# Sink values of two head pairs as two row tiles, and q and k loaded in rows of four tokens, in a fused attention and channel-mix kernel

## The chip, the cores and the metric

The kernel runs on one core of a Trainium2 chip. The metric is device time in microseconds for one execution, as the median of several runs; less is better. The engines are named as in the profile: PE is TensorE, DVE is VectorE, ACT is ScalarE, POOL is GpSimd, SP is SyncE (which issues nearly all DMAs). PEld is the weight load of TensorE, which overlaps its products.

## What is computed

Four batches of eight heads, 768 tokens, head size 64. Each token attends to the last 128 tokens up to itself and to four "sink" tokens at the start. The heads' outputs, side by side, are the 512 features of a channel mix with a shift by one token.

```python
def attention(q, k, v, n_sink=4, window=128):          # q, k, v: (4, 8, 768, 64)
    scores = q @ k.transpose(0, 1, 3, 2) / sqrt(64)
    rel = pos[:, None] - pos[None, :]
    keep = (pos[None, :] < n_sink) | ((rel >= 0) & (rel < window))
    a = softmax(where(keep, scores, -1e9))
    return a @ v

def channel_mix(x, mu_k, mu_r, w_k, w_v, w_r):          # x: (4, 768, 512)
    xk = mu_k * x + (1 - mu_k) * x_prev                 # x_prev: x one token earlier
    xr = mu_r * x + (1 - mu_r) * x_prev
    k = maximum(xk @ w_k, 0)                            # (512, 1024)
    return sigmoid(xr @ w_r) * (k * k @ w_v)            # (512, 512), (1024, 512)
```

All inputs and the output are float32; inside, the products are in bfloat16.

## The kernel before

**Units.** The work is cut into 12 units: a batch `b` and a block `T` of 256 tokens, `u = 3 b + T`. A unit is prepared (`prepare`), attended (`attend`), turned and mixed (`mix`), and sent through the two weight matrices and the gate (`ffn`). Stages of neighbouring units overlap.

**Preparation.** SP loads q, k and v in float32 (`load`). A cast makes them bfloat16 (`kb`, `qb` at L587 and L590, `vb` at L638). Then q and k are turned, so that head size lies on partitions and tokens along the row. For the units in `KD` (k of units 4 to 11) and `QD` (q of units 8 to 11) SP issues DMA transposes (L603). For the others TensorE transposes into a PSUM bank (L616) and ACT or DVE copies to `kt` or `qt` (L624). These last units load two tokens of a head as one row of 512 bytes (L403): partition `p` holds tokens `2p` and `2p + 1`, and the copy at L624 puts them in order by writing with a step of two. The others and v load rows of 256 bytes (L386, L396).

**Attention.** Heads are taken two at a time, as four "chunks" `c`. The scores (L701) use TensorE as two row tiles of 64 rows, one for each head of the chunk, and two chunks follow each other (`TOGETHER`). ACT takes the exponent (L737) and DVE multiplies with the window mask (L751). For blocks `T > 0` the sinks are computed apart: `sink_scores` (L678) gives the scores of all eight heads with their four sinks in one bank, on column tiles of 32; ACT makes `es` of it (L685), whose rows `32 c` to `32 c + 31` belong to chunk `c`. `vsink` holds the sinks' values, with zeros wherever row and head don't belong together, so that a product over all 128 rows of `es` gives the right sum for a chunk. `values` issues for each chunk and each half `g` of the tokens this sink product (L763) and then the products with the window's values (L775), all into one PSUM bank. DVE divides by the sum (L788, L791).

**Mix and weights.** `mix` transposes x on TensorE (L814), copies it out (L823), subtracts the shifted x (L841) and forms xk and xr (L852, all DVE). `ffn` issues the product with w_k (L902), the relu (L912 on ACT, L916 on DVE), the square (L924), the gate (L933), its tanh on ACT (L939), the product with w_v (L951) and the last multiplication on DVE (L960); L967 stores. The last half block has its own form (L872, L882). The weights are loaded at the start and cast (L552 to L558).

**What sets the order.** All operations are recorded in a `Plan`, each with a number. `ORDER` lists for every engine by hand which number follows which. `CHOICE` says for the operations that may run on several engines (casts, copies out of PSUM, relu) which engine takes them. `schedule` walks along these lists with costs written into the kernel, gives out the buffers and puts "fill" products (L971, `warm`) into gaps of TensorE in the first 22 us, which only keep it busy. On the chip every engine works its own list strictly in order, so an instruction that waits holds up everything behind it. PSUM has eight banks: four for the two score tiles and a pool of four, `bank`, for everything else.

Of the kernel before, what the change touches and what calls it, by code (L numbers as in the profile page):

```python
# [9 lines left out]
BF16 = mybir.dt.bfloat16  # L10
AX = mybir.AxisListType
AF = mybir.ActivationFunctionType
ALU = mybir.AluOpType
# [5 lines left out]
    79: "ACT", 82: "ACT", 83: "ACT", 85: "ACT", 87: "ACT", 89: "DVE", 94: "DVE", 95:  # L19
    "DVE", 97: "DVE", 101: "DVE", 102: "DVE", 128: "DVE", 134: "DVE", 136: "DVE", 137:  # L20
    "DVE", 140: "ACT", 141: "DVE", 150: "DVE", 191: "DVE", 192: "ACT", 193: "ACT", 218:
    "DVE", 265: "DVE", 273: "DVE", 278: "DVE", 305: "DVE", 343: "DVE", 346: "DVE", 348:
    "DVE", 352: "ACT", 354: "DVE", 361: "DVE", 423: "DVE", 429: "ACT", 430: "ACT", 499:
    "DVE", 501: "DVE", 504: "DVE", 507: "DVE", 508: "ACT", 520: "DVE", 586: "ACT", 587:
    "ACT", 654: "DVE", 658: "DVE", 660: "DVE", 663: "DVE", 672: "DVE", 736: "DVE", 738:
    "ACT", 739: "DVE", 744: "DVE", 751: "DVE", 815: "DVE", 816: "ACT", 825: "DVE", 885:
    "DVE", 887: "DVE", 891: "ACT", 892: "ACT", 1003: "DVE",
# [13 lines left out]
TOGETHER = 2  # L41

SWITCH = 100.0
# [8 lines left out]
        90, 93, 106, 96, 99, 104, 117, 77, 109, 114, 132, 138, 142, 129, 125, 120, 156,  # L52
        135, 158, 149, 184, 190, 169, 236, 208, 209, 212, 213, 220, 221, 161, 166, 172,
        177, 216, 194, 181, 201, 217, 187, 238, 291, 299, 292, 295, 300, 303, 249, 304,
        226, 296, 241, 246, 307, 224, 228, 277, 232, 229, 252, 261, 233, 267, 257, 311,
        264, 284, 270, 312, 319, 344, 309, 315, 330, 316, 349, 367, 375, 368, 376, 322,
        371, 395, 327, 372, 333, 338, 397, 275, 353, 379, 360, 380, 383, 408, 385, 387,
        422, 388, 445, 453, 446, 454, 400, 427, 405, 475, 411, 416, 391, 431, 392, 457,
        438, 458, 449, 473, 486, 450, 463, 526, 530, 527, 531, 500, 538, 461, 505, 539,
        469, 510, 470, 554, 478, 483, 534, 494, 489, 535, 512, 565, 557, 465, 579, 466,  # L60
        542, 519, 544, 562, 550, 584, 573, 551, 588, 546, 568, 632, 602, 547, 603, 606,
        614, 607, 595, 630, 643, 615, 620, 610, 618, 611, 640, 635, 678, 682, 679, 683,
        664, 646, 690, 706, 708, 686, 651, 687, 691, 626, 671, 719, 711, 622, 627, 694,
        623, 761, 757, 765, 758, 762, 766, 722, 696, 741, 727, 716, 775, 785, 702, 750,
        769, 743, 770, 796, 703, 788, 793, 698, 773, 699, 817, 777, 781, 778, 782, 835,
        831, 839, 832, 836, 799, 840, 859, 861, 843, 804, 847, 844, 824, 855, 849, 869,
        864, 872, 856, 907, 915, 908, 851, 916, 852, 880, 875, 911, 893, 912, 919, 900,
        920, 935, 937, 923, 925, 931, 948, 932, 973, 940, 974, 981, 945, 982, 951, 977,
        959, 978, 956, 985, 927, 966, 986, 928, 991, 989, 1001, 1009, 1005, 1002, 1013,
        1006, 1014, 1010, 993, 1021, 997, 994, 998, 1017, 1019, 1022, 1029, 1025, 1030,  # L70
        1026,
    ),
    "DVE": (
        69, 70, 89, 94, 95, 101, 97, 108, 102, 113, 110, 115, 111, 78, 137, 105, 116, 119,
        128, 124, 144, 126, 121, 134, 122, 127, 136, 150, 145, 151, 152, 146, 153, 191,
        147, 160, 148, 165, 80, 81, 154, 171, 141, 176, 162, 163, 167, 173, 168, 178, 174,
        179, 155, 196, 197, 203, 198, 205, 204, 211, 218, 199, 223, 206, 207, 84, 240,
        245, 305, 200, 86, 242, 306, 243, 247, 215, 248, 256, 219, 88, 278, 251, 294, 298,
        279, 230, 253, 302, 254, 234, 258, 259, 280, 265, 343, 286, 348, 281, 282, 287,
        289, 346, 321, 288, 313, 326, 317, 273, 337, 290, 323, 332, 324, 328, 283, 329,  # L80
        334, 339, 335, 340, 370, 354, 276, 374, 355, 361, 358, 362, 382, 356, 378, 364,
        357, 363, 423, 389, 399, 404, 410, 401, 415, 406, 402, 366, 412, 417, 407, 418,
        413, 359, 365, 448, 433, 393, 434, 440, 435, 442, 441, 456, 460, 499, 482, 477,
        504, 452, 529, 501, 488, 507, 436, 493, 511, 437, 471, 479, 480, 484, 444, 485,
        495, 556, 496, 490, 541, 491, 443, 537, 558, 572, 514, 559, 561, 533, 467, 515,
        520, 563, 521, 564, 517, 567, 574, 522, 575, 516, 523, 590, 552, 569, 591, 570,
        518, 525, 548, 524, 654, 634, 593, 639, 597, 660, 599, 658, 592, 598, 605, 645,
        636, 641, 637, 642, 650, 600, 617, 601, 613, 666, 647, 594, 609, 648, 652, 710,
        653, 669, 663, 667, 693, 668, 712, 672, 673, 675, 674, 676, 713, 628, 681, 624,
        670, 736, 721, 715, 726, 723, 724, 677, 685, 728, 729, 689, 760, 717, 742, 718,  # L90
        764, 792, 787, 751, 768, 739, 744, 789, 790, 794, 745, 704, 795, 746, 772, 752,
        748, 803, 747, 754, 753, 755, 700, 819, 779, 783, 798, 820, 749, 822, 834, 800,
        756, 801, 838, 805, 806, 815, 863, 842, 868, 825, 826, 821, 846, 827, 865, 828,
        866, 870, 885, 857, 823, 879, 887, 871, 829, 874, 853, 876, 881, 882, 877, 910,
        830, 918, 895, 898, 914, 902, 896, 922, 903, 939, 904, 944, 897, 933, 950, 941,
        942, 946, 947, 952, 955, 953, 905, 957, 958, 899, 961, 962, 906, 968, 976, 963,
        970, 969, 929, 980, 964, 972, 988, 984, 1003, 965, 1004, 1008, 971, 1012, 1016,
        995, 999, 1023, 1031, 1027,
    ),
    "ACT": (  # L100
        67, 68, 92, 91, 98, 112, 107, 100, 118, 131, 123, 133, 143, 139, 130, 183, 189,
        164, 159, 185, 79, 157, 175, 170, 82, 140, 210, 222, 237, 214, 180, 186, 195, 202,
        182, 192, 188, 244, 239, 293, 83, 301, 193, 255, 227, 250, 85, 297, 308, 87, 225,
        260, 266, 262, 263, 269, 268, 285, 271, 341, 325, 320, 345, 310, 336, 331, 350,
        369, 377, 396, 373, 419, 403, 398, 381, 421, 384, 424, 409, 386, 414, 352, 426,
        447, 455, 428, 481, 476, 432, 497, 439, 429, 502, 459, 451, 474, 487, 464, 528,
        532, 430, 492, 462, 506, 540, 560, 555, 508, 578, 536, 513, 571, 576, 580, 581,
        583, 543, 545, 566, 585, 586, 589, 638, 633, 604, 587, 656, 596, 608, 616, 631,
        621, 644, 619, 612, 649, 680, 684, 665, 707, 709, 714, 688, 692, 732, 730, 720,
        734, 695, 725, 738, 759, 767, 763, 697, 776, 791, 786, 771, 809, 797, 807, 802,  # L110
        774, 813, 811, 818, 833, 837, 841, 860, 862, 867, 845, 848, 816, 883, 850, 878,
        873, 889, 909, 917, 894, 913, 901, 936, 921, 938, 943, 891, 924, 892, 926, 949,
        975, 954, 983, 960, 967, 987, 979, 992, 990, 1007, 1015, 1011, 1020, 1018,
    ),
    "POOL": (
        72, 71, 73, 74, 75, 103, 76, 274, 272, 351, 509, 662, 740,
    ),
    "SP": (
        0, 1, 2, 3, 4, 5, 7, 6, 16, 8, 9, 10, 11, 15, 17, 12, 18, 13, 14, 19, 20, 25, 23,
        24, 21, 235, 22, 342, 347, 28, 30, 29, 314, 26, 27, 420, 425, 31, 231, 33, 34, 35,  # L120
        32, 498, 36, 318, 503, 37, 40, 38, 390, 39, 45, 394, 41, 577, 582, 42, 468, 43,
        44, 46, 47, 655, 657, 661, 659, 549, 48, 51, 49, 50, 472, 53, 52, 733, 731, 735,
        737, 54, 629, 57, 58, 55, 553, 56, 625, 810, 808, 705, 814, 812, 59, 60, 61, 780,
        63, 64, 62, 701, 884, 886, 890, 888, 65, 858, 66, 854, 934, 930, 784, 996, 1000,
        1024, 1032, 1028,
    ),
}


class Plan:  # L130

# [159 lines left out]
def kernel(  # L296
# [79 lines left out]
    def by_dma(name, u):  # L376
        return u in (KD if name == "k" else QD)

    def load(u, names, rank, h0=0, h1=H):
        b, T = divmod(u, NT)  # L380
        for name in names:
# [11 lines left out]
            if by_dma(name, u):  # L393
                for g in range(2):
# [5 lines left out]
                        hold=[key] if g else [], writes=[(name, u, g)])  # L400
                continue

            P.op("SP", 400.0 + 20.0 * (h1 - h0), lambda key=key, src=src: nc.sync.dma_start(  # L403
                out=buf[key][:, h0:h1, :, :].rearrange("p h j d -> p h (j d)"),
                in_=src[b, h0:h1, 256 * T:256 * T + 256, :].rearrange(
                    "h (p j) d -> p h (j d)", j=2)), rank,
# [617 lines left out]
```

## Time and profile before

| what | value |
|---|---|
| median of 3 runs | 171.35 us (170.58 to 173.37) |
| span of the profiled execution | 172.5 us |
| PE / DVE / ACT / POOL busy | 160.6 / 153.6 / 129.2 / 13.4 us |
| mean granted TensorE clock | 0.980 |
| read from HBM / written | 24.12 MB / 6.29 MB |
| sink products L763 | 64, 12.4 us busy |
| loads in rows of 512 B (L403) | 14 DMAs |
| casts on POOL (L638) | 3, 853 ns each |

The profile is of one execution, which is not one of the three runs that the median is of; its time is known by its span alone, 1.15 us above the median. Busy time of an engine counts instructions from start to end; products on TensorE overlap, so what one of them costs the stream is the distance between two starts.

### The profile page before, as it was taken

What the parts mean: (1) busy time and instruction counts of PE and PEld (TensorE: products, weight loads), DVE (VectorE), ACT (ScalarE), POOL (GpSimd) and SP (SyncE); (2) the same over time, 40 slices, a digit from 0 to 9 for tenths busy, and PEclk for the clock granted to TensorE, in tenths of its full rate; (3) what the DMA queues carried; (4) which work ended last, traced back from release to release, by engine and by line L of the source; (5) the groups of instructions that cost most, each with busy time, mean ns of one, the idle gap of its engine ahead of it and who ended that gap; (6) DMA issues with size and microseconds to landing.
All of it is one profiled execution on the core that took longest, in us unless ns stands there. A gap on an engine that the chain in (4) does not pass through costs nothing.

```text
span 172.5 us, 4178 instructions
## 1 busy us (share of the span) xinstructions
PE 160.6 (93%) x1588; PEld 106.3 (62%) x1605; DVE 153.6 (89%) x404; ACT 129.2 (75%) x208; POOL 13.4 (8%) x32
## 2 busy tenths in 40 slices
PE   7986869799999999999999999999999997999992
PEld 2444547675647667777567786756476773777551
DVE  6279895999999999999999999999999999699542
ACT  2488895999898999898979987865838958853320
POOL 7330000000010010050000200120000000000000
PEclk9999678999999999999999999999999999999999
DMA  4999999999156969999679489869969857102033
GB/s 144 243 302 365 291 254 353 380 298 229 26 139 157 287 124 240 197 257 289 163 170 226 96 212 243 159 170 212 240 149 256 213 111 211 61 4 113 11 122 122
DMA packets 81763, 33.82 MB, mean 196 GB/s; under 512 B 63688, under 2 KB 76240, under 8 KB 81744
## 3 DMA queue, kind: packets, MB, share of 16 engines
q1 hardware_dynamic: 81728, 33.56, 78.0%
q8 instruction: 12, 0.20, 0.6%
q14 instruction: 7, 0.06, 0.1%
q10 hardware_dynamic: 16, 0.00, 0.0%
HBM read 24.12 MB, written 6.29 MB: 176 GB/s over the span
## 4 chain that ended last, share of the span: by engine, by line
PE 82%; DVE 10%; DMA 3%; ACT 2%; issue 1%; DVEq 0%; ACTq 0%
PE bank L951 23%; PE bank L902 23%; PE bank L933 12%; PE sc L701 6%; PE bank L775 6%; PE bank L971 4%; PE bank L814 3%; DMA kt<-kb 3%; DVE e L751 2%; PE bank L616 2%; PE bank L763 2%; DVE xk L852 2%; ACT rl L912 1%; ACT e L737 1%; DVE x L791 1%
## 5 line engine op out<-in xcount | busy, mean ns | idle before, releaser
L902 PE MATMUL bank<-xk,wk_sb 128*128 128x256 bf16 x384 | 52.0, 278 | 1.6 <-DVE wk_sb L558 1.3
L737 ACT ACTIVATE e<-sc 128x1024 bf16<-128x1024 f32 (+1 forms) x48 | 44.5, 964 | 4.0 <-PE sc L701 4.0
L951 PE MATMUL bank<-wv_h,kk 128*128 128x512 bf16 x174 | 44.9, 379 | 0.7 <-issue 0.3
L902 PEld LDWEIGHTS <-wk_sb 128*128 128x128 bf16 x384 | 36.1, 100 | 10.2 <-DVE wk_sb L558 1.6
L912 ACT ACTIVATE rl<-bank 128x512 bf16<-128x512 f32 x45 | 26.2, 608 | 12.2 <-PE bank L902 9.6
L751 DVE TENSOR_TENSOR e<-e,mask 128x1024 bf16<-128x1024 bf16 (+1 forms) x48 | 30.0, 637 | 0.7 <-ACT e L737 0.7
L951 PEld LDWEIGHTS <-kk 128*128 128x128 bf16 x184 | 16.7, 98 | 15.8 <-issue 0.7
L933 PE MATMUL bank<-wr_sb,xr 128*128 128x512 bf16 x89 | 23.6, 379 | 0.3
L852 DVE SCALAR_TENSOR_TENSOR xk<-td,mu_all,xt 128x256 bf16<-128x256 bf16 x48 | 22.4, 491 | 0.1
L852 DVE SCALAR_TENSOR_TENSOR xr<-td,mu_all,xt 128x256 bf16<-128x256 bf16 x48 | 22.4, 476 | 0.0
L939 ACT ACTIVATE th<-bank 128x512 f32<-128x512 f32 x24 | 14.7, 618 | 7.8 <-PE bank L933 7.7
L960 DVE SCALAR_TENSOR_TENSOR ob<-th,bank 128x512 f32<-128x512 f32 x23 | 15.6, 680 | 5.6 <-ACT th L939 3.5
L791 DVE TENSOR_TENSOR x<-bank,rec 128x256 bf16<-128x256 f32 x48 | 19.4, 416 | 0.4
L924 DVE TENSOR_TENSOR kk<-rl 128x512 bf16<-128x512 bf16 x48 | 19.4, 415 | 0.1
L775 PE MATMUL bank<-vb,e 128*128 128x65 bf16 x352 | 18.9, 193 | 0.2
L775 PEld LDWEIGHTS <-e 128*128 128x128 bf16 x352 | 16.4, 98 | 3.0 <-DVE e L751 0.7
L701 PE MATMUL sc<-qt,kt 64*128 64x128 bf16 (+1 forms) x256 | 15.0, 246 | 1.7 <-DMA kt<-kb 0.9
L701 PEld LDWEIGHTS <-kt 64*128 64x128 bf16 x256 | 9.4, 97 | 7.9 <-issue 3.4
L933 PEld LDWEIGHTS <-xr 128*128 128x128 bf16 x96 | 8.9, 98 | 8.5 <-issue 0.3
L763 PE MATMUL bank<-vsink,es 128*128 128x130 bf16 x64 | 12.4, 220 | 0.4 <-ACT rl L912 0.3
L823 ACT COPY xt<-bank 128x512 bf16<-128x512 bf16 x15 | 8.8, 586 | 5.3 <-PE bank L814 5.1
L788 DVE RECIPROCAL rec<-bank 128x4 f32<-128x4 f32 x48 | 8.0, 174 | 3.2 <-ACT rl L912 1.8
(67 smaller groups left out, 166.5 us busy)
## 6 DMA issues: line engine op xcount, KB each, us to landing
vs<-in_v_dram SPq DMA_DIRECT2D x24, 256.0 KB, 3.9
out_dram<-ob SPq DMA_DIRECT2D x23, 256.0 KB, 3.2
ks<-in_k_dram SPq DMA_DIRECT2D x18, 256.0 KB, 4.7
qs<-in_q_dram SPq DMA_DIRECT2D x7, 512.0 KB, 9.5
qs<-in_q_dram SPq DMA_DIRECT2D x10, 256.0 KB, 5.4
w<-in_moe_w_k_dram SPq DMA_DIRECT2D x2, 1024.0 KB, 9.2
w<-in_moe_w_v_dram SPq DMA_DIRECT2D x2, 1024.0 KB, 9.9
ks<-in_k_dram SPq DMA_DIRECT2D x3, 512.0 KB, 8.0
```

Of the source, the lines that this page charges most:

```text
L701: nc.tensor.matmul(out=sc[:, a, o0:o1], lhsT=lhs[rows], rhs=rhs[rows], start=u not in BIAS, stop=True, skip_group_check=u in BIAS)
L737: nc.scalar.activation(out=buf[ek][:, :, lo:], in_=buf[sck][:, :, lo:], func=AF.Exp, scale=scale)
L751: nc.vector.tensor_tensor(out=at, in0=at, in1=m, op=ALU.mult)
L763: nc.tensor.matmul(out=o[:, g, :, :], lhsT=buf["es", u][:, 128 * g:128 * g + 128], rhs=vsink[b % 2][:, 2 * c:2 * c + 2, :], start=True, st ...
L775: nc.tensor.matmul(out=o[:, g, a, :], lhsT=e[:, a, e0:e0 + 128], rhs=rhs, start=(T == 0 and i == 0), stop=(i == len(blocks) - 1), skip_gro ...
L791: P.op("DVE", dve(256), lambda ok=ok, rk=rk, c=c: nc.vector.tensor_tensor(out=buf["x", u][:, :, 128 * c:128 * c + 128].rearrange("p g (a d ...
L852: nc.vector.scalar_tensor_tensor(out=buf[key][:, c0 + i, :], in0=buf[tk][:, i, :], scalar=mu[w][:, c0 + i:c0 + i + 1], in1=xt[:, c0 + i, t ...
L902: nc.tensor.matmul(out=ps[:, i, :], lhsT=wk_sb[:, c, 128 * f:128 * f + 128], rhs=xk[:, c, :], start=(c == 0), stop=(c == NC - 1), skip_gro ...
L912: nc.scalar.activation(out=buf[rk], in_=buf[psk].rearrange("p (i t) -> p i t", i=2), func=AF.Relu)
L924: P.op("DVE", dve(512, 0.52), lambda f2=f2, rk=rk: nc.vector.tensor_tensor(out=buf["kk", u][:, 2 * f2:2 * f2 + 2, :], in0=buf[rk], in1=buf ...
L933: nc.tensor.matmul(out=buf[psk], lhsT=buf["xr", u][:, c, 128 * g:128 * g + 128], rhs=wr_sb[:, c, :], start=(c == 0), stop=(c == NC - 1))
L951: nc.tensor.matmul(out=buf[psk], rhs=wv_h[:, f, :], lhsT=buf["kk", u][:, f, 128 * g:128 * g + 128], start=(f == 0), stop=(f == NF - 1))
```

## The change

The change has three parts.

1. The sink products leave `values` and become an operation of their own, `sink_values`, for two chunks together. Each chunk uses only the half of `es` and `vsink` that its rows lie in (64 rows), so the two chunks' products run on two row tiles of TensorE, into two banks. To have a chunk from each half in a pair, the chunks are taken in the order 0, 2, 1, 3 (`CHUNK`).
2. q and k of the units that TensorE transposes are loaded with four tokens of a head as one row of 1 KB: partition `64 w + p` holds tokens `4p` to `4p + 3` of the four heads `4 w` to `4 w + 3`. This takes two DMAs, one for each `w`, of 64 partitions each, where there was one of 128. The casts, the transposes and the copies follow; the copy to `kt` or `qt` writes with a step of four.
3. `ORDER` and `CHOICE` are new throughout. By the two programs, 14 casts of q and k go to POOL, which had none, POOL has two casts of v for three, and there are 22 fill products for 24.

The core of the diff; the lists `ORDER` and `CHOICE` are left out, and so are changes of index in `mix` and of keys that follow from the new order of chunks:

```diff
+CHUNK = (0, 2, 1, 3)
...
-            P.op("SP", 400.0 + 20.0 * (h1 - h0), lambda key=key, src=src: nc.sync.dma_start(
-                out=buf[key][:, h0:h1, :, :].rearrange("p h j d -> p h (j d)"),
-                in_=src[b, h0:h1, 256 * T:256 * T + 256, :].rearrange(
-                    "h (p j) d -> p h (j d)", j=2)), rank,
...
+            rows = src[b, :, 256 * T:256 * T + 256, :].rearrange(
+                "(w l) (p j) d -> w p l (j d)", w=2, j=4)
+            c0, c1 = h0 // 4, h1 // 4
+            for w in range(2):
+                P.op("SP", 400.0 + 20.0 * (c1 - c0), lambda key=key, rows=rows, w=w: (
+                    nc.sync.dma_start(
+                        out=buf[key][64 * w:64 * w + 64, h0:h1].rearrange(
+                            "p (l x) j d -> p l (x j d)", x=2),
+                        in_=rows[w][:, 2 * c0:2 * c1])), rank,
...
             def evacuate(copy, half=half, psk=psk, key=key):
                 return lambda: copy(
-                    out=buf[key][:, 2 * half:2 * half + 2, :, :].rearrange(
-                        "p c g (t j) -> p c j (g t)", j=2),
+                    out=buf[key][:, half::2, :, :].rearrange(
+                        "p c g (t j) -> p c j (g t)", j=4),
...
+                if T > 0:
+
+                    def sink_values(cs=cs):
+                        for g in range(2):
+                            for r, i in enumerate(cs):
+                                rows = slice(64 * r, 64 * r + 64)
+                                o = buf["o", u, i][:, 130 * g:130 * g + 130]
+                                nc.tensor.matmul(
+                                    out=o.rearrange("p (a d) -> p a d", a=2),
+                                    lhsT=buf["es", u][rows, 128 * g:128 * g + 128],
+                                    rhs=vsink[b % 2][rows, 2 * CHUNK[i]:2 * CHUNK[i] + 2, :],
+                                    start=(g == 0), stop=False, skip_group_check=True)
+
+                    P.op("PE", 114.0, sink_values, r + 1, lag=PE_LAG, mode=1,
+                         take=[("bank", ("o", u, i)) for i in cs], hold=[("es", u)],
+                         writes=[("os", u, i) for i in cs], reads=[("es", u), ("vsink", b % 2)])
...
                 for g in range(2):
-                    if T > 0:
-                        nc.tensor.matmul(out=o[:, g, :, :],
-                                         lhsT=buf["es", u][:, 128 * g:128 * g + 128],
-                                         rhs=vsink[b % 2][:, 2 * c:2 * c + 2, :],
-                                         start=True, stop=False, skip_group_check=True)
                     for a in range(2):
```

## The prediction

> **What bounds the kernel now.** I read the page's busy row first, then the windows, then the chain, and last the rows of what the change touches.
>
> ```profile
> span 172.5 us, 4178 instructions
> PE 160.6 (93%) x1588; PEld 106.3 (62%) x1605; DVE 153.6 (89%) x404; ACT 129.2 (75%) x208; POOL 13.4 (8%) x32
> ```
>
> ```profile
> 20.00:35.00 15.00, 11.60 (x125) 8.80 (x125) 13.04 (x33) 12.40 (x21) 0.00 (x0) 0.86 1.06 315
> 35.00:50.00 15.00, 14.84 (x145) 9.22 (x147) 14.97 (x38) 14.36 (x24) 1.11 (x3) 1.00 0.78 179
> ...
> 95.00:110.00 15.00, 14.89 (x162) 10.49 (x163) 14.93 (x42) 13.15 (x22) 1.14 (x1) 1.00 0.88 187
> ...
> 140.00:155.00 15.00, 13.95 (x155) 9.93 (x154) 12.93 (x36) 10.83 (x18) 0.00 (x0) 1.00 0.36 98
> ```
>
> The windows give busy us of PE, weight loads, DVE, ACT and POOL, the granted clock, the DMA share and GB/s. From 35 to 140 both TensorE and VectorE are full (14.8 to 15.0 of every 15 us in the rows to 110). An edit there must be charged to both, and one engine's gain is worth nothing if the other grows. Before 35 us no engine is full and DMA is (1.06). After 140 VectorE has slack: 2.07 us in the last row, while TensorE has 1.05.
>
> ```profile
> PE 82%; DVE 10%; DMA 3%; ACT 2%; issue 1%; DVEq 0%; ACTq 0%
> ```
>
> The chain that ended last agrees: TensorE for 82%, VectorE for 10%. In time order its VectorE pieces stand mainly between 10.4 and 24 us (masks, casts, the xk products, the cast of wk_sb), and its largest DMA piece is a 4.50 us transpose into kt at 139.08.
>
> **Part 1, the sink values on TensorE.** In the timeline:
>
> ```profile
> 65.74 0.28 PE L775 MATMUL bank<-vb,e 128*128 128x65 bf16 x4
> 65.95 0.62 PE L701 MATMUL sc<-qt,kt 64*128 64x256 bf16 x12
> 66.50 0.23 PE L763 MATMUL bank<-vsink,es 128*128 128x130 bf16 x1
> 66.57 0.28 PE L775 MATMUL bank<-vb,e 128*128 128x65 bf16 x4
> 66.69 0.22 PE L763 MATMUL bank<-vsink,es 128*128 128x130 bf16 x1
> ```
>
> Durations overlap, so I go by starts. A sink product holds the stream for 0.06 to 0.07 us (66.50 to 66.57), and it and four value products take 0.18 to 0.19 (66.50 to 66.69), so 0.03 for each value product. I take 0.057 for the sink, 130 columns at the pace of L902, whose four of 256 columns take 0.44 us in the chain. 64 of them are 3.65 us. Two row tiles at once halve that, **-1.82 us**. The scores show that row tiles run side by side: 12 of them have 2048 columns, which one after the other would be 0.87 us, and the block takes 0.55.
>
> But those scores also price the change of tile shape. Four value products from 65.74 end at 65.86, and the scores begin at 65.95: 0.09 us to go in. Their 1024 column steps are 0.44, the block takes 0.55: 0.11 to come out. About 0.095 for each boundary. Counting boundaries between full, 64-row and 32-column blocks in the two orders of instructions gives 58 before and 73 after, because only about half of the 16 new sink blocks stand beside scores. 15 x 0.095 = **+1.42**. So part 1 is -0.4 us, with bounds of -1.8 (boundaries free) and +1.4 (no concurrency). The blocks also take two of the four PSUM banks earlier than the products did; whatever waits for a bank then stands at the head of TensorE's queue. I cost that at nothing, as the new order places the block just ahead of its values, often beside scores; without that cover it is one bank's drain, 0.4 (the x product) for a block.
>
> **Part 2, the orders: casts go to POOL.** By the two orders, 14 casts of q and k move to POOL and it loses one of v. VectorE loses 3 casts, 2 copies of qt and one of xt, and its other swaps cancel (one relu and one wv_h cast more, one wk_sb cast less): by the chain's steps 3 x 0.34 + 2 x 0.64 + 0.34 - 0.62 = 2.0 us less. ScalarE loses about 4.8 us (11 casts at 0.62 less, two copies of qt at 0.76 and one each of xt and vb more, and swaps that nearly cancel). It is not what ends the chain (2%), so I give that no value. What POOL's work costs VectorE can be read where POOL casts now:
>
> ```profile
> 61.59 0.81 POOL L638 CAST vb<-vs 128x512 bf16<-128x512 f32 x1 [13.28 <-DMA vs<-in_v_dram]
> 73.76 2.44 POOL L655 COPY ksink<-kt 64x16 bf16<-64x16 bf16 x2 [11.36 <-DMA kt<-kb]
> 96.49 1.14 POOL L638 CAST vb<-vs 128x512 bf16<-128x512 f32 x1 [20.29 <-DMA vs<-in_v_dram]
> ```
>
> ```profile
> 61.45 1.62 DVE L852 SCALAR_TENSOR_TENSOR xk<-td,mu_all,xt 128x256 bf16<-128x256 bf16 x3
> ```
>
> Three such products take 1.28 us at 19.82; beside POOL's cast they take 1.62, +0.34. The pair at 97.07 takes 1.23 against 0.88 elsewhere, +0.35, and a cast at 47.89 0.71 against 0.41, +0.30. I take 0.33 for each of 13 more casts, +4.3 us on VectorE, **+2.3** with what it loses. The bounds for one cast are 0 (it meets an operation that needs no shared path) and 0.85, the mean of POOL's three. Of the 2.3 us I let 1.5 fall into VectorE's 2.07 us of slack between 140 and 155, where it waits for the late kt: **+0.8** on the end; without that cover 2.3. The 73.76 row is the other side: two tiny copies took 2.44 us behind masks on VectorE, where others take 0.2 each. A POOL cast that comes 2 us late delays its TensorE transpose, and everything behind that in TensorE's fixed order. These casts are mostly a unit ahead: I take **+0.5** in all, bounds 0 and +2.
>
> The Trainium skill (SBUF — State Buffer, "Who interferes with whom") says that the pair of ports that VectorE shares with GpSimd is an exclusive lock, held for the whole instruction, the loser blocking fully. The rows show the loss but less than a whole cast; by the rule, 13 x 0.85 less 2.0 would be +9 us on VectorE and not +2.3.
>
> **Part 3, loads in 1 KB rows.** Twelve loads of 512 KB go from 1024 rows of 512 B to 512 rows of 1 KB, each as two DMAs of 64 partitions. Nothing in the trace fills half the partitions. Three windows (9.5 to 13, 29 to 35, 100 to 110 us) show what whole ones do, with rows mainly of 512 B, 2 KB and 256 B:
>
> ```profile
> DMA packets 2074, 1.05 MB, mean 299 GB/s; under 512 B 32, under 2 KB 2074, under 8 KB 2074
> ...
> DMA packets 1534, 2.23 MB, mean 372 GB/s; under 512 B 128, under 2 KB 577, under 8 KB 1532
> ...
> DMA packets 7131, 2.26 MB, mean 226 GB/s; under 512 B 6873, under 2 KB 6873, under 8 KB 7129
> ```
>
> A load takes 1.75 us at 299, 1.41 at 372, and 3.5 if half the partitions give half the rate. So a load changes by -0.34 to +1.75. Five of them stand ahead of the first wk. That is issued at 9.02 and 11.0 and lands a median 9.2 later, about 18.2 and 20.2; ScalarE casts it from 20.49, VectorE at 23.62: 2.3 us of cover. I take **0**, in the middle of the short side, since longer rows were faster in every window, and expect neither to reach the end.
>
> On SP 14 DMAs are added (28 for 14) at 0.36 to 0.5 us each, some 6 us. Queued behind them are the v loads, the stores and the DMA transposes of kt and qt. The first eight matter: the first half of k needs the third issue instead of the first, about 0.9 us later; it is cast at 3.87 now, but TensorE does not transpose it before 6.65, since 12 filling products stand ahead. After has 11 there, and 22 in all for 24; at 0.43 that is up to -0.85, and I take **-0.4**. The copies of kt and qt now write with a step of four elements for two. The step of two already costs ScalarE 0.15 to 0.17 over a plain copy (737 to 757 against 586 ns); another 0.15 x 19 there would be 2.9 us, hidden in its idle 25%. I take 0.
>
> The Trainium skill (SBUF — State Buffer, "Door 1: The DMA port swizzle") measures 196 GB/s for 64 partitions against 328 for 128 at 1 MiB, and two DMAs on the two halves only 6% above one. No row here shows it. By it (estimate) a load would take 1.75 x 328/196 = 2.9 us, the wk would come 5 x 1.18 = 5.9 us late, 3.6 beyond its cover.
>
> **Sum**: 172.5 - 0.4 + 0.8 + 0.5 + 0 - 0.4 = 173.0 for the span. The profiled span lies 1.15 us above the median of the runs (171.35), so I take the +0.5 to the median: 171.9, said as **172.0**. About 2% is what a measurement of this kernel can tell from no change; that is 167.9 to 174.8.
>
> **Rivals.**
> *VectorE pays for POOL* (the slower one). Place: VectorE between 35 and 110, where it has no idle time. At 0.6 for a cast, 13 x 0.6 - 2.0 - 1.5 = +4.3 instead of 0.8, so 175.4; at 0.85, 178.7. It passes 2% from about 0.55. For it: 61 to 73 us above, and no slack. Against: 0.30 to 0.35 in all three cases. Chance 0.19.
> *Half-filled loads are slow.* Below about 237 GB/s five loads eat the 2.3 us of cover; at half of 299 the first keys start 8.75 - 2.3 = 6.5 late, 178; midway to that, about 175. For it: DMA is full before 35. Against: 1 KB rows, and the same bytes. Chance 0.11.
> *The new order wins the start* (faster). The start holds 24 fills, 8.8 us busy, and seven TensorE waits of 0.2 to 1.31 us, 4.2 together; at 140 another 1 us goes to the kt transpose. Two fills, two thirds of the waits and that one: 0.85 + 2.8 + 1.0 = -4.7, so 167.2. Against: between 10 and 24 us the chain runs over VectorE, which gets POOL's collisions there. Chance 0.20.
> *The row tiles don't run side by side*: +1.4 for -0.4, 173.8. Chance 0.02, as scores do.
>
> **Numbers.** The forecast keeps 0.48. Faster 0.20; within 2% 0.48 + 0.02 = 0.50; slower 0.19 + 0.11 = 0.30. The range runs from 167.0 to 177.5, into each side case, leaving out about 0.1 on either side.
>
> **What would show it.** Right: sink products starting in pairs, 16 blocks near 0.12 us of stream, boundaries of 0.09 to 0.11; VectorE still full from 35 to 140 with stretched operations of +0.3 beside POOL's casts; POOL at about 24 us; the 9.5 to 13 us rate near 300 GB/s or above. Wrong: TensorE waiting on POOL's kb or qb in the middle; a rate near 190 in the start and keys waiting for wk_sb; VectorE busy above 158; or keys beginning two microseconds earlier.

## The result and the profile after

The changed kernel takes 178.37 us (177.93 to 178.44); the kernel before took 171.50 beside it. The ratio is 1.041, 95% interval 1.037 to 1.044: slower, and above the 177.5 us at which the prediction's range ended. (Ratios here compare undisturbed runs only, so they need not equal the quotient of two medians.) The profiled execution took 178.31 us, with a span of 176.6 for 172.5. In every run on record the time is about 1.7 us above the span, so the profile of before, with its span of 172.5, stands for an execution of about 174.2 us (an estimate), 2.7 above the median: the two profiles show 4.1 of the 6.9 us that the medians differ by.

Its page, busy time first, and the chain that ended last:

```profile
span 176.6 us, 4238 instructions
...
PE 161.1 (91%) x1603; PEld 102.9 (58%) x1603; DVE 157.1 (89%) x399; ACT 134.6 (76%) x200; POOL 19.7 (11%) x45
...
PE 55%; ACT 16%; DMA 8%; DVE 8%; SPq 6%; issue 3%; POOL 0%; DVEq 0%; ACTq 0%; POOLq 0%
```

TensorE is as busy as before (161.1 for 160.6), so 3.6 of the 4.1 us are new idle time: 15.5 us outside its busy time for 11.9. ScalarE gained 5.4 us, where 4.8 us less were expected. In the chain ScalarE went from 2% to 16%, DMA from 3% to 8%, and SP's issuing is new with 6%. The windows say where:

```profile
20.00:35.00 15.00, 10.43 (x139) 7.67 (x137) 14.05 (x35) 14.98 (x20) 0.61 (x1) 1.00 1.06 302
35.00:50.00 15.00, 13.70 (x127) 7.88 (x125) 14.42 (x33) 13.69 (x20) 2.38 (x3) 1.00 1.04 231
95.00:110.00 15.00, 15.00 (x182) 10.98 (x181) 14.93 (x41) 14.36 (x25) 0.00 (x0) 1.00 0.94 197
140.00:155.00 15.00, 15.00 (x170) 9.97 (x168) 14.30 (x39) 11.86 (x20) 0.00 (x0) 1.00 0.44 117
```

The engines stand in the order TensorE, weight loads, VectorE, ScalarE, POOL. ScalarE is busy 14.98 of 15 us between 20 and 35, where it had 12.40, while TensorE fell from 11.60 to 10.43 (part of that is its clock: granted 1.00 for 0.86, it ran 139 products for 125). In the last two rows TensorE has no idle time at all. The loss is made in the first third: over the first 50 us TensorE is busy for 39.2 us where it had 43.3. The chain in time order (start, length, what) shows by what:

```profile
0.81 0.73 SPq L418
...
1.60 0.60 SPq L418
...
9.07 0.62 SPq L418
...
9.73 5.72 DMA ks<-in_k_dram
...
20.71 1.31 ACT kt L639
22.02 0.85 ACT wk_sb L568
22.87 1.20 ACT qt L639
24.06 0.85 ACT e L768
...
31.96 1.93 ACT kt L639 x2
...
35.74 0.60 SPq L418
...
39.09 8.96 DMA qs<-in_q_dram
...
48.17 0.48 issue
48.65 1.30 ACT qt L639
```

Three things stand in it that were costed at nothing: SP's issues of q and k, the loads themselves, and the copies to kt and qt on ScalarE. The last in the groups (busy us, mean ns of one; L639 was L624, where ScalarE's copies took 737 to 757 ns and VectorE's 725 to 728):

```profile
L639 ACT COPY qt<-bank 128x512 bf16<-128x512 bf16 x13 | 17.3, 1333 | 2.9 <-PE bank L631 2.9
L639 ACT COPY kt<-bank 128x512 bf16<-128x512 bf16 x6 | 7.7, 1322 | 4.1 <-PE bank L631 4.1
L639 DVE COPY qt<-bank 128x512 bf16<-128x512 bf16 x3 | 3.9, 1294 | 0.5 <-PE bank L631 0.5
```

And the loads, in the stretch from 9.5 to 13 us that the prediction used (its first row of before said 299 GB/s), with the two loads of w_k that follow (9.2 us to landing before):

```profile
DMA packets 1075, 0.81 MB, mean 231 GB/s; under 512 B 363, under 2 KB 1075, under 8 KB 1075
...
w<-in_moe_w_k_dram SPq DMA_DIRECT2D x2, 1024.0 KB, 12.2
```

A packet of 1 KB took a median 79 ns between 10 and 15 us; one of 512 B took 33 before. The second load of w_k landed at 24.53 for 20.74. The first product with w_k starts at 22.9 us, for 22.0 before.

### The profile page after: what moved, and what is told of

Same layout as the page of the kernel before. It is cut to its first block, busy times and chain, and to the rows that moved or that the text cites. A ratio compares the mean times of both kernels' runs of the same rounds, so it can differ in the third digit from the quotient of the medians.

```text
span 176.6 us, 4238 instructions
## 1 busy us (share of the span) xinstructions
PE 161.1 (91%) x1603; PEld 102.9 (58%) x1603; DVE 157.1 (89%) x399; ACT 134.6 (76%) x200; POOL 19.7 (11%) x45
## 4 chain that ended last, share of the span: by engine, by line
PE 55%; ACT 16%; DMA 8%; DVE 8%; SPq 6%; issue 3%; POOL 0%; DVEq 0%; ACTq 0%; POOLq 0%
PE bank L930 16%; PE bank L979 16%; PE bank L961 8%; SPq L418 6%; DMA qs<-in_q_dram 5%; ACT qt L639 5%; PE bank L801 5%; ACT e L768 5%; PE sc L716 4%; DMA ks<-in_k_dram 3%; DVE xr L879 2%; PE bank L841 2%; ACT kt L639 2%; PE bank L756 2%; ACT xt L850 1%
## 5 line engine op out<-in xcount | busy, mean ns | idle before, releaser
L930 PE MATMUL bank<-xk,wk_sb 128*128 128x256 bf16 x384 | 51.0, 273 | 2.6 <-ACT wk_sb L568 1.7
L768 ACT ACTIVATE e<-sc 128x1024 bf16<-128x1024 f32 (+1 forms) x48 | 45.5, 978 | 3.4 <-PE sc L716 3.4
L979 PE MATMUL bank<-wv_h,kk 128*128 128x512 bf16 x184 | 46.4, 379 | 0.1
L930 PEld LDWEIGHTS <-wk_sb 128*128 128x128 bf16 x384 | 35.5, 98 | 13.1 <-issue 2.3
L961 PE MATMUL bank<-wr_sb,xr 128*128 128x512 bf16 x96 | 24.2, 379 | 0.1
L879 DVE SCALAR_TENSOR_TENSOR xr<-td,mu_all,xt 128x256 bf16<-128x256 bf16 x48 | 22.9, 492 | 0.1
L818 DVE TENSOR_TENSOR x<-bank,rec 128x256 bf16<-128x256 f32 x48 | 19.4, 418 | 0.5
L639 ACT COPY qt<-bank 128x512 bf16<-128x512 bf16 x13 | 17.3, 1333 | 2.9 <-PE bank L631 2.9
L801 PE MATMUL bank<-vb,e 128*128 128x65 bf16 x352 | 16.2, 193 | 2.0 <-DVE e L782 2.0
L801 PEld LDWEIGHTS <-e 128*128 128x128 bf16 x352 | 13.8, 97 | 5.3 <-DVE e L782 2.3
L850 ACT COPY xt<-bank 128x512 bf16<-128x512 bf16 x16 | 9.5, 594 | 2.3 <-PE bank L841 2.2
L868 DVE TENSOR_TENSOR td<-xt 128x512 bf16<-128x512 bf16 x24 | 10.2, 434 | 0.8 <-ACT xt L850 0.8
```

What stands on the lines that cost most here:

```text
L639: return lambda: copy(out=buf[key][:, half::2, :, :].rearrange("p c g (t j) -> p c j (g t)", j=4), in_=buf[psk].bitcast(BF16)[:, 0:512].re ...
L768: nc.scalar.activation(out=buf[ek][:, :, lo:], in_=buf[sck][:, :, lo:], func=AF.Exp, scale=scale)
L801: nc.tensor.matmul(out=o[:, g, a, :], lhsT=e[:, a, e0:e0 + 128], rhs=rhs, start=(T == 0 and i == 0), stop=(i == len(blocks) - 1), skip_gro ...
L818: P.op("DVE", dve(256), lambda ok=ok, rk=rk, c=c: nc.vector.tensor_tensor(out=buf["x", u][:, :, 128 * c:128 * c + 128].rearrange("p g (a d ...
L879: nc.vector.scalar_tensor_tensor(out=buf[key][:, c0 + 2 * i, :], in0=buf[tk][:, i, :], scalar=mu[w][:, c0 + 2 * i:c0 + 2 * i + 1], in1=xt[ ...
L930: nc.tensor.matmul(out=ps[:, i, :], lhsT=wk_sb[:, c, 128 * f:128 * f + 128], rhs=xk[:, c, :], start=(c == 0), stop=(c == NC - 1), skip_gro ...
```

## The experiments

Two theories stood against each other at first: **copies** (the step of four on ScalarE) and **loads** (64 partitions for a DMA, or rows of 1 KB). A third said that neither matters and POOL's casts or the new order lost the time. The runs were taken in several batches; each ratio is to runs of the kernel before from the same batch, whose median went from 171.50 to 172.72 us, so medians of different batches are less comparable than ratios.

**e1, copies without a step.** The tokens are left in another order, so this prices the walk alone.

```diff
-  out=...rearrange("p c g (t j) -> p c j (g t)", j=4),
+  out=...rearrange("p c g (j t) -> p c (g j) t", j=2),
```

> The changed kernel with one thing taken away: the copies from PSUM to kt and qt write without a step, so the tokens stay in the order of the transpose (that part of the computation is left out). Loads, casts, orders, sinks and all counts stay. In the changed kernel these 24 copies take 1.3 us each, against 0.73 to 0.76 before. Theory 'copies' (the step of four is what costs): ScalarE, full from 20 to 65 us, gets 19 x 0.7 us back, the copies take 0.59 on ScalarE and about 0.42 on VectorE, and the time falls to 171 to 174. Theory 'loads' (half-filled 1 KB loads at 229 GB/s, and 28 of them, are what costs): the start still waits for q, k and the weights, 176 to 178. Theory 'POOL' (its casts and the new order): 177 to 178.5.

Measured: 175.92 us, ratio 1.024 (1.017 to 1.031); ScalarE's busy time fell from 134.6 to 123.4:

```profile
L639 ACT COPY qt<-bank 128x512 bf16<-128x512 bf16 x13 | 7.7, 592 | 4.4 <-PE bank L631 4.4
L639 ACT COPY kt<-bank 128x512 bf16<-128x512 bf16 x6 | 3.4, 595 | 4.2 <-PE bank L631 4.2
L639 DVE COPY qt<-bank 128x512 bf16<-128x512 bf16 x3 | 1.3, 422 | 0.9 <-PE bank L631 0.8
```

Taking 0.74 us from every copy on ScalarE (0.87 on VectorE) gives back 2.5 us; 4 remain.

**e2, the same copy walked the other way:** it writes in order and reads PSUM with a step instead. That step is one transposed block, 128 elements, in runs of four.

```diff
-  out=..."p c g (t j) -> p c j (g t)", in_=..."p (j c t) -> p c j t"
+  out=..."p c g (t j) -> p c (g t) j", in_=..."p (j c t) -> p c t j"
```

> The changed kernel with the same copies walking the other way: they write kt and qt in order and read PSUM with a step of one transposed block, the same elements to the same places. If the price sits in the stepped write, a copy falls to 0.6 to 0.75 us and the time to 171 to 174 as in the kernel without a step. If it sits in reading PSUM in short pieces or in two-byte elements as such, the copy stays at 1.3 or grows and the time stays at 177 to 180. Under 'loads' and 'POOL' it is 176 to 178.5 whatever the copies take.

Measured: 176.22 us, 1.024 (1.016 to 1.032). ScalarE's copies take 0.59 us, VectorE's 0.69. So the price sits in the stepped write. Read this way, the order of the result costs ScalarE nothing and VectorE 0.27 us (0.42 in e1).

**e3, the row form undone:** rows of 512 bytes over all 128 partitions and copies with a step of two, as before; still two DMAs for a load (four heads each), and all else as changed; the casts and the transposes follow the layout.

```diff
-  rows = ...rearrange("(w l) (p j) d -> w p l (j d)", w=2, j=4)
+  rows = ...rearrange("(w l) (p j) d -> p w l (j d)", w=2, j=2)
...
-  out=buf[key][64 * w:64 * w + 64, h0:h1]...
+  out=buf[key]...[:, w, 2 * c0:2 * c1]
```

> The changed kernel with part 2 undone and the rest kept: rows of 512 bytes over all 128 partitions, still two DMAs for a load (four heads each), the copies write with a step of two as before. Row-tile sinks, the new orders and POOL's casts stay. 'Copies': copies at 0.74, 171 to 174. 'Loads': DMA at about 299 GB/s in 10 to 15 us instead of 229, wk landing earlier by about 2 us, 171 to 174 too; the two are told apart by the kernel without a step, which keeps the loads. 'POOL': 176 to 178.5.

Measured: 172.72 us, 1.003 (0.999 to 1.008), and the rate between 9.5 and 13 us is back:

```profile
DMA packets 2077, 1.03 MB, mean 295 GB/s; under 512 B 63, under 2 KB 2077, under 8 KB 2077
```

The row form, with its loads and its copies, is the whole loss. Sinks in pairs, POOL's casts and the new orders together are worth nothing that can be measured. The third theory falls.

**e4, the kernel before with copies of a step of four** (tokens left in another order).

```diff
-  out=..."p c g (t j) -> p c j (g t)", j=2
+  out=..."p c g (t j) -> p c j (g t)", j=4
```

> The kernel before with one thing added: its copies to kt and qt write with a step of four instead of two (so tokens are shuffled within a unit; that part of the computation is wrong). Everything else is the kernel before. 'Copies': 24 copies at 1.3 instead of 0.74, 17 of them on ScalarE, and the time rises by 3 to 6 us to 174.5 to 177.5. 'Loads' and 'POOL': within 1 us of before, 171 to 172.5.

Measured: 180.48 us, 1.049 (1.042 to 1.056), copies 1.33 us. One changed number in an access pattern costs the old order 8 us. Why the old order suffers more than the new one (e14 below) is not shown. The traces show one difference: between 20 and 30 us TensorE was granted 0.51 of its clock here, 0.80 in the kernel before and 0.96 in e14. How much of the 8 us that is, no run tells.

**e5, half partitions without long rows:** e3, but a whole load's two DMAs take 64 partitions and eight heads each.

```diff
-  out=buf[key]...[:, w, 2 * c0:2 * c1], in_=rows[:, w, 2 * c0:2 * c1]
+  out=buf[key][64 * w:64 * w + 64]..., in_=src[b, :, 256 * T + 128 * w:256 * T + 128 * w + 128, :]...
```

> The kernel with part 2's row form undone (rows of 512 bytes, copies with a step of two; 172.72 us, 1.0034 of the kernel before), but each whole load's two DMAs are split as in the change: 64 partitions each, all eight heads, instead of all partitions and four heads each. Half partitions: the rate between 10 and 15 us falls from 300 to about 230 GB/s, a packet of 512 bytes takes near 40 ns for 30, wk lands about 12 us after its issue, and the time is 175 to 176.5. Row length (the rows of 1 KB were slow, whatever the partitions): about 300 GB/s and 172 to 173.5.

Measured: 177.05 us, 1.036 (1.030 to 1.043); packets of 512 B a median 42 ns for 29 in e3. The rate between 9.5 and 13 us, and the chain by engine:

```profile
DMA packets 1612, 0.80 MB, mean 229 GB/s; under 512 B 48, under 2 KB 1612, under 8 KB 1612
...
PE 51%; DVE 21%; DMA 12%; SPq 9%; issue 3%; ACT 1%; POOL 0%; DVEq 0%; POOLq 0%
```

The same bytes in the same rows lose over a fifth of their rate when each DMA fills half the partitions. This alone costs 4.3 us by the medians, and ScalarE has 1% of the chain. One thing is left open: e1 and e2 have half-filled loads too and are at 1.024. Their copies are 0.15 us shorter and their rows longer; which of the two makes the difference, no run separates.

**e6, the kernel before with e2's edit.**

> The kernel before, with one edit: the copies to kt and qt write in order and read PSUM with a step of two, instead of writing with the step. The copies fall from 0.74-0.76 to 0.59 us on ScalarE (24 copies, most there), from 0.73 to about 0.6 on VectorE. If ScalarE's copies sat on the way to the end in the kernel before too, 169.5 to 171 (ratio 0.985 to 0.993); if its idle quarter hid them, ratio 0.995 to 1.003. A step of four cost this kernel 8 us, about 0.4 us for each 0.59 us of a copy; by that proportion 0.15 a copy would be worth 2 us.

Measured: 172.25 us, 1.002 (0.998 to 1.006), copies 0.59 and 0.68 us. In the kernel before, 0.15 us a copy was hidden, as the prediction had said of it; by the interval no more than 0.4 us of it can have shown.

**e7, e3 with the sink products as before** (128 rows, at the head of each chunk's values).

```diff
-  sink_values: lhsT=es[64 r:64 r + 64, ...], rhs=vsink[64 r:64 r + 64, ...], two chunks side by side
+  values: lhsT=es[:, ...], rhs=vsink[:, ...], start=True
```

> The kernel of 172.72 us (the change without its row form), with part 1 undone as well: the sink products are again products of all 128 rows at the head of each chunk's values, and the paired blocks are gone; the bank is still taken at the block's place. By the sum of the prediction part 1 is worth -0.4 us (64 products of 0.057 us halved, 15 boundaries of 0.095 added), so this kernel is 0.4 slower, ratio 1.003 to 1.010, with a sink product at 0.055 to 0.07 us of stream. If the boundaries cost nothing it is 1.8 us slower (1.014); if the pairs bring nothing it is 1.4 faster (0.995).

Measured: 172.04 us, 1.007 (1.003 to 1.012). The interval overlaps that of e3, and by the medians alone it is e7 that is faster, by 0.7 us.

**e9, e3 with e2's walk and one DMA for a whole load.**

> The kernel of 172.72 us (rows of 512 bytes), with two edits: its copies to kt and qt write in order and read PSUM with the step, and a whole load is one DMA over all partitions instead of two. Copies theory: 0.15 us less for each of the copies, at the price measured between the step of four and the plain copy (2.5 us for 0.72 a copy), -0.5 us. Loads theory: nine or more DMA issues fewer on SP at 0.5 us each; the loads' own rate stays 300 GB/s; -0.3 to -1 at the start. Together 171 to 172.3, ratio 0.992 to 1.000. If neither lies on the way to the end, 1.003 as before.

Measured: 170.64 us, 0.998 (0.995 to 1.002): the best form of the new orders, and no different from the kernel before.

**e8 and e10, from e9:** the first moves the 14 casts of q and k from POOL to ScalarE, the second undoes the sink pairs.

> The best form so far of the new orders (rows of 512 bytes, copies that write in order, one DMA for a whole load; 170.64 us, ratio 0.998) with the 14 casts of q and k that the change gave to POOL moved to ScalarE, each at its place in time. The prediction charged POOL's casts 1.3 us on the end (0.8 for VectorE operations stretched by 0.33 each, 0.5 for POOL being late). If that holds and ScalarE hides 14 x 0.62 us, 169.3 to 170, ratio 0.990 to 0.995. If ScalarE, which is full from 20 to 35 us (14.84 of 15), has to pay there for the casts, 171 to 173, ratio 1.001 to 1.012, and then POOL's casts bought something.

> The same best form (170.64 us, ratio 0.998) with part 1 undone: each sink product again over all 128 rows at the head of its chunk's values. The first such pair of kernels gave 1.0074 with full products against 1.0034 with pairs, with intervals that overlap. By the prediction's sum 0.4 us slower, ratio 1.000 to 1.004. If boundaries between tile shapes cost nothing, 1.8 slower (1.008); if the pairs bring nothing, 1.4 faster (0.990).

Measured: e8 171.06 us, 1.001 (0.996 to 1.005), VectorE's busy time 152.0 for 153.2, ScalarE's 129.7 for 123.2. e10 170.93 us, 0.999 (0.995 to 1.003). Both lie 0.3 to 0.4 us above e9 by their medians, within the intervals.

**e11, rows of 1 KB over all partitions:** from e2, one row to each of 128 partitions for a DMA, four DMAs for a load.

```diff
-  rows = "(w l) (p j) d -> w p l (j d)"    # a DMA: one w, 64 partitions
+  rows = "(w l) (p j) d -> l w p (j d)"    # a DMA: one l, 128 partitions
```

> The changed kernel with its rows of 1 KB and steps of four, with two edits: the copies write in order and read PSUM with the step (this alone gave 176.22 us, 1.0242), and each DMA of q or k moves one row of 1 KB to every one of the 128 partitions (heads l and l + 4, for l from 0 to 3), instead of four rows to each of 64; a whole load is four DMAs instead of two. Half partitions: the rate between 10 and 15 us rises from 229 to 300 GB/s or above, packets of 1 KB take near 50 to 60 ns instead of 79, and the time is 171 to 173, less whatever the longer rows bring, plus some 10 us more of issuing on SP over the whole kernel that may show as SP waits. Row length: 229 GB/s still, and 176.

Measured: 273.73 us. The DMA view between 10 and 15 us:

```profile
DMA packets 240, 0.24 MB, mean 48 GB/s; under 512 B 4, under 2 KB 240, under 8 KB 240
...
q1 hardware_dynamic: 240, 0.24, 13.6%
```

13.6% of 16 DMA engines is 2.2 of them, and a packet takes 46 ns: about two engines did all the work. The Trainium skill (DMA: Bandwidth & Descriptors, "Rules for kernel authors") says that an outermost dimension smaller than 16 confines a DMA to at most so many engines; the source here has the two heads outermost, and the trace agrees. The run says nothing about long rows.

**e12, the kernel before with whole loads split over partition halves.**

> The kernel before, with one edit: every whole load of q or k in rows of 512 bytes (ten of them) is two DMAs of 64 partitions each instead of one of 128. Half partitions: 230 GB/s between 10 and 15 us instead of 313, SP's issues 0.6 us each; the changed orders lost 4.3 us by this edit, so 174.5 to 177.5 here, ratio 1.015 to 1.035. If the new orders alone were sensitive to it (more of their loads stand ahead of wk), 171.5 to 174.

Measured: 173.75 us, ratio 1.015 (0.991 to 1.040), inconclusive. The rate between 10 and 15 us fell from 313 to 232 GB/s, and the second load of w_k landed at 23.83 for 20.74. In its profile the products with w_k are no later for it: the first at 22.1 us for 22.0, the 65th of the 384 at 52.1 for 52.4. So that half-filled loads cost time is shown for the new orders only.

**e13, e11 with the 64 row groups outermost** (head l on the even partitions, head l + 4 on the odd ones).

```diff
-  "(w l) (p j) d -> l w p (j d)"
+  "(w l) (p j) d -> l p w (j d)"
```

> The changed kernel with rows of 1 KB, copies that write in order and read PSUM with the step, and each DMA of q or k moving one row to each of the 128 partitions, now with head l on the even and head l + 4 on the odd partitions, so that the DMA's outermost dimension is 64 tokens' rows and not two heads. Four DMAs for a whole load. If half partitions are the cause and the row's length is harmless: 300 GB/s or more between 10 and 15 us, 1 KB packets of 46 to 60 ns, 170 to 172.5, ratio 0.997 to 1.008, less if the added issues on SP (some 0.5 us each) hold up v. If rows of 1 KB are slow themselves: 230 GB/s and 175 to 176.5. If the packets come one after the other again, far above 200.

Measured: 175.62 us, 1.021 (1.014 to 1.027). The packets are at their 46 ns again (median, 10 to 15 us), so rows of 1 KB are not slow at this load, which leaves the DMA engines partly idle. For the rate is no better (9.5 to 13 us):

```profile
DMA packets 1012, 0.79 MB, mean 226 GB/s; under 512 B 284, under 2 KB 1012, under 8 KB 1012
...
q1 hardware_dynamic: 1012, 0.79, 84.9%
```

The chain shows what limits it: SP, 0.60 us for each DMA, 12 in a row from 7.31 to 15.40, each of 128 KB.

```profile
14.15 0.60 SPq L418
14.75 0.04 issue
14.80 0.60 SPq L418
15.40 0.04 issue
15.44 6.04 DMA w<-in_moe_w_k_dram
```

128 KB every 0.65 us is 202 GB/s; the w_k is issued at 15.44 instead of 11.70. The repair traded one limit for another.

**e14, e3 with a step of four** (the edit of e4, tokens left in another order).

> The kernel of 172.72 us (new orders and row tiles, rows of 512 bytes over all partitions) with one edit: the copies to kt and qt write with a step of four instead of two, which leaves the tokens in another order. Copies 1.31 us for 0.74. If the two losses add up, the loads being 4.3 (177.05 less 172.72) and all of it 5.7, this gives 1.3 to 2.4 more, 174 to 175.1, ratio 1.011 to 1.020. If the copies' price was partly hidden behind the late loads, more: 176 to 178, ratio 1.025 to 1.035. If ScalarE's idle time hides them when the loads are in time, as the prediction had it, 172.7.

Measured: 177.70 us, 1.030 (1.025 to 1.036). The chain by engine and the same stretch of it as above:

```profile
PE 63%; ACT 21%; DVE 10%; issue 4%; DVEq 0%
```

```profile
20.81 1.31 ACT kt L641
22.12 0.85 ACT wk_sb L567
22.96 1.21 ACT qt L641
24.17 0.85 ACT e L770
```

No DMA and no SP is left in the chain, and the copies alone cost 5.0 us by the medians. With e3, e5 and the changed kernel this makes a table:

| | step of two | step of four |
|---|---|---|
| 128 partitions | 172.72 (e3) | 177.70 (e14) |
| 64 partitions | 177.05 (e5) | 178.37 (after, rows of 1 KB) |

The losses are 5.0 and 4.3 us, and 5.7 together. The four come from different batches; by their ratios to the kernel before they are 2.7%, 3.3% and 3.7%, or 4.6, 5.6 and 6.4 us. Which of the two is the larger is not shown, but either way both together cost far less than their sum: they lie beside each other, not one behind the other. The trace says where: the first of the 384 products with w_k starts at 20.2 us in e3, 23.0 in e14, 21.8 in e5 and 22.9 in the changed kernel; the 65th at 51.7, 54.1, 55.5 and 54.9; the 128th at 70.8, 74.8, 74.2 and 74.8. The copies are late by 2.8 us at the first product already; the loads by 1.6 there and by 3.9 at the 65th; at the 128th each alone has lost 3.4 to 4.0 us, and both lose 4.0. (The profile of e5 is of the longest of its four runs, with a granted clock of 0.50 from 15 to 20 us and 0.89 from 35 to 50, for 0.66 and 1.00 in e3; part of its lateness is that.) That is why e1 gave back only 2.5 and e14, read as the changed kernel with its loads mended, only 0.7.

## Why the prediction was wrong

**The copies (the step that failed first).** "[A]nother 0.15 x 19 there would be 2.9 us, hidden in its idle 25%. I take 0." Both halves are wrong. The price was taken as linear in the step, from 0.59 without one to 0.74 with two; with four it is 1.32 to 1.34, +0.57 to 0.59 a copy, 11 us on ScalarE and not 2.9. And the 25% is a mean over the span. ScalarE had 2.6 us free between 20 and 35 in the kernel before (12.40 of 15). In the changed kernel five of its copies start in that stretch, 5 x 0.58 = 2.9 us more, and its list is in order: the casts to wk_sb, the exponents and the relus wait behind each copy. For 0.15 a copy the cover did hold (e6). No rival spoke of this.

**The loads (the step that failed second).** "I take 0, in the middle of the short side, since longer rows were faster in every window." The windows compared row lengths; the change also halved the partitions, and that was the part that mattered (e5: 229 GB/s for 295 with the rows left at 512 bytes). The rival of half-filled loads had the mechanism, at 0.11: it decides below 237 GB/s, and the trace shows 229 to 231. Its midway value, "about 175", is close to what e1 shows without the copies' price (175.92). The Trainium skill (SBUF — State Buffer, "Door 1: The DMA port swizzle") spoke against the change with 196 GB/s for 64 partitions and 328 for 128 at 1 MiB; the trace has 229 to 231 against 295 to 299 between 9.5 and 13 us, the same sign with a smaller gap. The prediction set a stated rule about exactly this shape behind a mean over other shapes.

**SP's issues.** The prediction took 0.36 to 0.5 us for each; 64-partition DMAs take 0.60, so v is issued at 6.15 us and not 2.96, and the w_k at 11.70 for 9.02. The "up to -0.85", taken as -0.4, for an earlier start of TensorE was not found: its gaps above 0.1 us between 0 and 40 add up to 9.7, where 6.2 stood before. The rival in which the new order wins the start (0.20) had something to it: with loads and copies mended (e9) the first product with w_k starts at 20.4 us for 22.0 and the 65th at 48.6 for 52.4. But the time does not follow (0.998). Some of that lead may lie in the profile of before, which is of a longer execution than its median.

**The sinks.** -0.4 with bounds of -1.8 and +1.4. In the medians of starts, the two products of a pair begin 4 ns apart; going on to a full-array block costs 0.093 us (148 ns to its first start, where 55 stand without a change of shape) and coming from one 0.096 (205 for 109), as the 0.095 said. By their ratios to the kernel before, e7 against e3 and e10 against e9 put the part at -0.7 and -0.2 us, inside their error; by the medians it is +0.7 and -0.3. The two prices in the sum are borne out, and the sum is too small to be seen. What the blocks cost by taking two banks early, which was put at nothing, is not tested: e7 and e10 still take the bank at the block's place. In five of the 16 blocks of the changed kernel the second product starts 0.2 to 0.4 us behind the first, 1.5 us in all, and in none of e3; what it waits for is not shown.

**POOL's casts.** One cast does cost what was read, where it meets a product with both inputs in SBUF (0.83 for 0.48, first two lines). The other way round POOL can be late: the cast in the last line took 2.75 us, where most took 0.61.

```profile
48.20 0.63 POOL L606 CAST qb<-qs 128x512 bf16<-128x512 f32 x1 [3.00 <-DMA qs<-in_q_dram]
48.27 0.83 DVE L879 SCALAR_TENSOR_TENSOR xk<-td,mu_all,xt 128x256 bf16<-128x256 bf16 x1
...
77.81 2.75 POOL L653 CAST vb<-vs 128x512 bf16<-128x512 f32 x1 [2.86 <-DVE ob L988]
```

But many meet operations with an input in PSUM, and those lost nothing (L818 took 0.39 to 0.42 us beside six of the casts, and 0.42 on average). Taking the casts off POOL gave VectorE back 1.2 us (e8), not 4.3, and the time did not improve. The +1.3 on the end was too much; the rival built on it was nowhere near. Of VectorE's +3.5 us in the changed kernel, the dearer step of its five copies (1.29 for 0.73) is 2.8. POOL was busy for 19.7 us, where 24 had been expected.

**Two slips that moved nothing.** The changes listed for ScalarE add up to 4.1 us less and not 4.8, and e3 shows 4.1 (125.1 for 129.2); no part of the sum rested on it. The profiled execution of before was put 1.15 us above the median by holding its span against a time; it is 2.7, but the sum took only the +0.5 to the median.

## What to carry to other kernels

A step in an output is priced by its size: measure or bound the new step, not the old one scaled. Look for an engine's free time in the stretch where the added work will stand, and ask what follows it in that engine's list. When two faults delay the same point, mending one shows little: run the fourth cell of the table before calling a cause small.

## What the runs showed of the hardware

- Writing 128x512 bf16 from PSUM, ScalarE took 0.59 us in order, 0.74 to 0.76 with a step of two elements and 1.32 to 1.34 with four; VectorE 0.42, 0.73 and 1.29 to 1.30. Reading PSUM in runs of two or four elements that lie 128 apart, and writing in order, cost ScalarE next to nothing (0.59 to 0.62) and VectorE 0.26 (0.68 to 0.69). The Trainium skill (SBUF — State Buffer, "Door 1: The DMA port swizzle", the note on cachelines) holds two hits in a line of 16 bytes enough for full bandwidth, which a step of four bf16 elements still has. The runs do not agree: that step more than doubled the write.
- While loads of q and k into 64 partitions filled the queue (10 to 15 us), 227 to 237 GB/s, whether in rows of 512 B (42 ns a packet, e5 and e12) or 1 KB (75 to 79 ns, the changed kernel and e2); into 128 partitions 300 to 313 at 27 to 33 ns for 512 B.
- Where nothing held it up, SP mostly took 0.58 to 0.64 us to issue a DMA of 64 partitions or of 128 rows of 1 KB, 0.45 to 0.51 for one of 128 partitions with two or four rows of 512 B each.
- A DMA with an outermost dimension of two used about two of the 16 DMA engines, 48 GB/s.
